# Folding the later batches' softmax into w_in with seven half-size products in place of eight

## The chip, the cores and the metric

The kernel runs on one core of a Trainium2 chip. The metric is device time in microseconds (us) of one execution, the median of several runs. The program uses five engines that run side by side, each in its own program order: TensorE (PE in the profile, with its weight loads as PEld), VectorE (DVE), ScalarE (ACT), GpSimd (POOL, here an issuer of DMAs) and SyncE (SP, likewise).

## What is computed

The reference is an attention over channels followed by a feed-forward layer. Its core, with 4 batches of 6080 tokens, 256 channels and 2048 hidden columns:

```python
qn = q / (np.linalg.norm(q, axis=1, keepdims=True) + 1e-06)
kn = k / (np.linalg.norm(k, axis=1, keepdims=True) + 1e-06)
s = kn.transpose(0, 2, 1) @ qn / tau            # 256 x 256 for each batch
a = softmax(s, axis=-1)
x = (v @ a).reshape(B * N, 256)
h = x @ w_in                                    # 256 -> 2048
r = np.maximum(h, 0.0)
g = s_moe * (r * r) + b
out = g @ w_out                                 # 2048 -> 256
```

The kernel never forms `v @ a`. It multiplies the softmax of a batch into `w_in` once, `wa = a @ w_in` (256 x 2048), and then computes `h = v @ wa`. The product `a @ w_in` is called the fold here, and the fold of batches 1, 2 and 3 is what the change touches.

## The kernel before

One long loop goes through 48 groups of 512 tokens, 16 steps to a group. A step is one pass of the loop: two matmuls of 128x512 for the hidden columns of the group at hand (`mm1`), and seven matmuls of 128x128 for the output of the group before. That output is computed by a seven-product scheme of its own (`seven_items`), whose results VectorE evacuates. On odd steps ScalarE evacuates two hidden tiles through a ReLU.

```python
    for s in range(NS + FT):
        g, m = divmod(s, FT)                # FT = 16
        if g < NG:
            mm1(g, m)                       # PE: 2 x 128x512
        ...
        if work:
            items, n = work[0]
            for f in items[:n]:             # PE: 7 x 128x128 (n = 7); an evacuation on DVE after each product
                f()
        ...
        if g < NG and m % 2 == 1:
            relu(g, m // 2)                 # ACT, out of h_ps (ps_h has 2 buffers)
        if g < NG and g not in plain and m in SQUARES:
            square(g, *SQUARES[m])          # m = 3, 5: ACT, one tile each; m = 8, 12: DVE, two tiles each
        ...
        elif m == 0 and 0 < g and g - 1 not in plain:
            square(g - 1, 6, 8, nc.vector)
        elif 0 < g and g - 1 not in plain and m in SUMS:
            sums_of(g - 1, SUMS[m])         # DVE, m = 2, 3, 6, 10
        for f in side.pop(s, []):           # whatever was put at this step
            f()
```

Each engine keeps the order in which the loop issues its instructions. The work of the next batch (its gram matrix, norms, softmax and fold) is put into this loop with `at_step`, in the steps before its first group. The finishing part starts 54 steps ahead of a point three steps before that group; for batch 1 these are the steps from 120 on, with its first group beginning at step 176:

```python
    FIN = (0, 3, 5, 7, 9, 11, 13, 17, 19, 22)
    ...
        w1 = first_group[b] * FT - 3        # 173 for batch 1
        fin_len = 54
        ...
        def fin_step(gr=gr, s=w1 - fin_len):
            ops = gr.finish_ops()
            for i, f in enumerate(ops):
                at_step(int(s) + 1 + (FIN[i] if i < len(FIN) else FIN[-1] + 3 * (i - len(FIN) + 1)), f)
```

The first ten of these operations are the copy of the gram matrix, the norms, four activations for the inverse norms, the scaling, two exponentials and the row sums. Then comes the fold: four blocks of 512 columns, two output halves each, so eight items, three steps apart (145, 148, ... 166 for batch 1):

```python
            def scaled(f0, n, m, wa_ps):
                dst = self.wa[:, m, ds(f0, n)]
                if m == 0 and not (self.b == 0 and NW <= f0 < 3 * NW):
                    po(nc.scalar.mul(out=dst, in_=wa_ps, mul=st["rs"][:, m : m + 1]))
                else:
                    po(nc.vector.tensor_scalar_mul(
                        out=dst, in0=wa_ps, scalar1=st["rs"][:, m : m + 1]))

            def fold_mm(f0, n, m, wa_ps):
                for j in range(CH):                          # CH = 2
                    po(nc.tensor.matmul(wa_ps, st["e"][:, j, ts(m, P)],
                                        w_in16[:, j, ds(f0, n)],
                                        start=(j == 0), stop=(j == CH - 1)))

            def fold_one(f0, n, m):
                def f():
                    wa_ps = self.bank("wa_ps", CH, C).rearrange("p a c -> p (a c)")[:, :n]
                    fold_mm(f0, n, m, wa_ps)
                    scaled(f0, n, m, wa_ps)
                return f
```

For batches 1 to 3 `self.bank` takes its tile from `ps_gram`, a pool with one buffer. An item therefore can begin on TensorE only when the evacuation of the item before it has ended. Even items are evacuated by ScalarE, odd ones by VectorE.

Of the kernel before, what the change touches and what calls it, by code (L numbers as in the profile page):

```python
# [9 lines left out]
FP16 = mybir.dt.float16  # L10
FP32 = mybir.dt.float32
FP32R = mybir.dt.float32r
AF = mybir.ActivationFunctionType
ALU = mybir.AluOpType
# [3 lines left out]
def kernel(  # L18
# [12 lines left out]
    nc = tc.nc  # L31
    P = 128

    B, N, C = q.shape
    Dff = moe_w_in.shape[1]
# [20 lines left out]
    def po(ins):  # L56

        tc.keep_in_program_order(ins)
        return ins

    def pool(name, bufs, **kw):
        return ctx.enter_context(tc.tile_pool(name=name, bufs=bufs, **kw))
# [3 lines left out]
    wpool = pool("wpool", 1)  # L66
    qk_pool = pool("qk_pool", 8)
    sq_pool = pool("sq_pool", 2)
    late_pool = pool("late_pool", NLATE)
    f3_pool = pool("f3_pool", 13)  # L70
    sm_pool = pool("sm", 1)
    apool = pool("apool", 2)
# [3 lines left out]
    gpool = pool("gpool", 2)  # L76
    spool = pool("spool", 1)
    upool = pool("upool", 4)
    opool = pool("opool", 2)

    ps_gram = pool("ps_gram", 1, space=PSUM)
# [29 lines left out]
    class Gram:  # L111
# [45 lines left out]
        def norm_ops(self, c):  # L157

            qc, kc = self.tiles[c]
            _, np_, jc = self.chunks[c]  # L160
            st = {}

            at_end = self.b == 0 and c >= len(self.chunks) - NLATE

            def squares(a, js):
                def f():
                    if "sq" not in st:
                        st["sq"] = (late_pool if at_end else sq_pool).tile(
                            [P, 2, JC, C], FP16, tag="sq", name="sq")
                    if a == 1 and at_end and c == len(self.chunks) - 1:  # L170
                        po(nc.vector.tensor_mul(
                            st["sq"][:np_, 1, js, :], kc[:np_, js, :], kc[:np_, js, :]))
                    elif a == 0 and (self.b > 0 or at_end or c % 2 == 0):
                        po(nc.vector.tensor_mul(  # L174
                            st["sq"][:np_, 0, js, :], qc[:np_, js, :], qc[:np_, js, :]))
                    else:
                        po(nc.scalar.activation(  # L177
                            out=st["sq"][:np_, a, js, :], in_=(qc, kc)[a][:np_, js, :],
                            func=AF.Square))
                return f  # L180

            def fold(half, arrays, last):
                def f():
                    src = st["f", 2 * half] if 2 * half < jc else st["sq"]
                    if ("f", half) not in st:
                        if last:
                            t = f3_pool.tile([P, 2, 1, C], FP16, tag="f3", name="f3")
                        else:
                            t = sq_pool.tile([P, 2, half, C], FP16, tag=f"f{half}", name="f")
                        st["f", half] = t  # L190
                    po(nc.vector.tensor_add(  # L191
                        st["f", half][:np_, arrays], src[:np_, arrays, :half, :],
                        src[:np_, arrays, half : 2 * half, :]))
                    if last and c == 0:
                        self.first = st["f", half]
                    if last and (c == 0 or self.b > 0 and c == len(self.chunks) - 1):
                        for rows in self.rows:
                            rows.append((st["f", half], np_, 1))
                return f

            def into_first():

                dst, src = self.first[:np_], st["f", 1][:np_]
                if self.b == 0:
                    po(nc.vector.tensor_add(dst, dst, src))
                else:
                    po(nc.gpsimd.dma_start(out=dst, in_=src, accum_op=ALU.add))  # L207

            def unfolded(a):
                self.rows[a].append((st["sq"], np_, jc))  # L210

            ops = []
            for h in range(0, jc, 4):
                js = slice(h, min(h + 4, jc))
                ops += [squares(1, js), squares(0, js)]
            if at_end:
                def rows(a):
                    if a == 0 or jc == 2:
                        return unfolded(a)
                    half = sq_pool.tile([P, 2, 2, C], FP16, tag="f2", name="half")  # L220
                    po(nc.vector.tensor_add(half[:np_, 1], st["sq"][:np_, 1, :2], st["sq"][:np_, 1, 2:]))
                    self.rows[1].append((half, np_, 2))
                return ops + [rows]
            if jc == 8:
                ops += [fold(4, slice(0, 1), False), fold(4, slice(1, 2), False)]
            ops += [fold(2, slice(0, 2), False), fold(1, slice(0, 2), True)]
            return ops + [into_first] if 0 < c < len(self.chunks) - 1 else ops
# [24 lines left out]
        def finish_ops(self):  # L252
# [78 lines left out]
            def first_block(n):  # L331

                two = [self.bank("wa_ps", CH, C)[:, 0, :n], h_tile("wa_ps")[:, 0, :n]]
                r_ps = self.bank("r_ps", CH, C)[:, :, 0]
                for j in range(CH):
                    exps(j)
                    for ch in range(CH):
                        po(nc.tensor.matmul(r_ps[:, ch : ch + 1], st["e"][:, j, ts(ch, P)],
                                            parts16, start=(ch == 0 and j == 0),
                                            stop=(ch == CH - 1 and j == CH - 1),  # L340
                                            skip_group_check=True))
                    for m in range(CH):
                        po(nc.tensor.matmul(two[m], st["e"][:, j, ts(m, P)],
                                            w_in16[:, j, :n],
                                            start=(j == 0), stop=(j == CH - 1)))
                st["rs"] = sm_pool.tile([P, CH], FP32, tag="rs", name="rs")
                po(nc.vector.reciprocal(out=st["rs"], in_=r_ps))
                for f0 in range(0, n, P):
                    for m in range(CH):
                        scaled(f0, P, m, two[m][:, ds(f0, P)])  # L350
# [5 lines that stand above are left out]
                    scaled(f0, n, m, wa_ps)  # L356
                return f

            if self.b == 0:
                blocks = [(2 * P, 2 * P), (4 * P, 2 * P), (6 * P, 2 * P), (2 * NW, NW), (3 * NW, NW)]  # L360
            else:
                blocks = [(f0, NW) for f0 in range(0, Dff, NW)]
            folds = [fold_one(f0, n, m) for f0, n in blocks for m in range(CH)]
            if self.b == 0:
                return [norms(1), *inverse(1), norms(0), *inverse(0), lambda: scale(CH),
                        lambda: first_block(2 * P)] + folds
            return [copy_out, norms_both, *inverse(), scale, lambda: exps(0), lambda: exps(1),
                    sums] + folds

        def bank(self, name, a, b):  # L370

# [189 lines left out]
        po(nc.scalar.copy(out=T[:, ts(i, 2), :], in_=w[:, 0, :, :P] if T is T2 else w[:, 0, :, P:]))  # L561


    side, early = {}, {}

    def at_step(s, f):
        side.setdefault(int(s), []).append(f)
# [31 lines left out]
    for b in range(1, B):  # L599
        gr = grams[b]  # L600
        w0 = first_group[b - 1] * FT + (26 if b == 1 else 6)
        w1 = first_group[b] * FT - 3
        NCH = len(gr.chunks)
        fin_len = 54
        span = (w1 - fin_len) - w0 - 12
        n = NCH * JC
        for c in range(NCH):
            sc = w0 + span * c * JC / n
            at_step(max(3, sc - 16), lambda gr=gr, c=c: gr.load(c))
            if c == 0:  # L610
                at_step(sc, gr.start)
            for j in range(JC):
                at_step(w0 + span * (c * JC + j) / n, lambda gr=gr, c=c, j=j: gr.mm(c, j))

            def norm_step(gr=gr, c=c, sc=sc):
                ops = gr.norm_ops(c)
                for i, f in enumerate(ops):
                    at_step(int(sc) + 2 + 1 + i * 3, f)
            at_step(sc + 1, norm_step)

        def fin_step(gr=gr, s=w1 - fin_len):
            ops = gr.finish_ops()
            for i, f in enumerate(ops):
                at_step(int(s) + 1 + (FIN[i] if i < len(FIN) else FIN[-1] + 3 * (i - len(FIN) + 1)), f)
        at_step(w1 - fin_len - 12, fin_step)


# [292 lines left out]
```

## Time and profile before

The time is 718.22 us, the median of three runs (718.15 to 718.64). The profiled execution spans 716.3 us with a mean granted TensorE clock of 0.997.

| group of instructions, per the profile | count | mean ns of one |
|---|---|---|
| fold matmul, 128x512 (`wa_ps`) | 56 | 379 |
| hidden matmul, 128x512 (`h_ps`) | 1408 | 379 |
| ReLU, 128x1024, ACT | 376 | 1022 |
| square of a hidden tile, 128x1024, ACT | 93 | 1052 |
| scaled fold evacuation, 128x512, ACT | 13 | 683 |
| scaled fold evacuation, 128x512, DVE | 15 | 744 |
| output evacuation, 128x256, DVE | 138 + 138 + 46 | 481, 477, 482 |
| sum of two f16 tiles, 128x2048, DVE | 45 | 1215 |
| square or sum of f16 tiles, 128x1024, DVE | 39 (L174) | 683 |

A mean duration is the time from an instruction's start to its end. Instructions of one engine overlap a little, so the spacing from start to start in a busy stretch is shorter and is read from the timeline. This matters most on TensorE, where a 128x512 matmul lasts 379 ns in the records and the next one starts 216 ns later. A "releaser" is the instruction whose end let a waiting one go.

### The profile page before, as it was taken

To read this page: it belongs to the slowest core of one execution; us is meant where nothing else is said; L and a number is where in the kernel's file an instruction comes from. 1 tells how busy PE (TensorE), PEld (TensorE's weight loads), DVE (VectorE), ACT (ScalarE), POOL (GpSimd) and SP (SyncE) were. 2 spreads that over 40 slices of the span, in tenths; PEclk is the share of its full clock that TensorE was granted. 3 is DMA by queue.
4 is the path that set the end of the run, shared out by engine and by line. 5 is a ranking of instruction groups with operands and counts; after the bars stand their busy time and mean duration, and the time that the engine had idled before them with its cause. 6 is when DMAs were issued, how large, how long until landed. Compare 5 with 4: busy or idle time off the path is not lost.

```text
span 716.3 us, 17491 instructions
## 1 busy us (share of the span) xinstructions
PE 696.8 (97%) x7421; PEld 503.6 (70%) x7421; DVE 624.0 (87%) x877; ACT 544.7 (76%) x592; POOL 110.8 (15%) x189
## 2 busy tenths in 40 slices
PE   4699999999999999999999999999999999999998
PEld 2456777776677777777677777777668777777777
DVE  4889999988789989998889899998887888888886
ACT  5779877787777777778777778777877777777874
POOL 4532332102101222101010222110000000000000
PEclk9999999999999999999999999999999999999999
DMA  9999999636565978444672887843323333321201
GB/s 236 207 259 167 165 174 136 122 89 124 111 122 109 135 134 144 112 89 95 138 146 52 145 137 125 153 90 77 98 63 75 94 70 75 97 60 46 82 31 75
DMA packets 87454, 83.47 MB, mean 117 GB/s; under 512 B 56304, under 2 KB 62256, under 8 KB 87376
## 3 DMA queue, kind: packets, MB, share of 16 engines
q0 software_dynamic: 26608, 43.40, 37.7%
q1 hardware_dynamic: 60192, 37.64, 22.0%
q8 instruction: 58, 0.95, 0.6%
q10 hardware_dynamic: 576, 1.31, 0.5%
q14 instruction: 20, 0.16, 0.1%
HBM read 78.91 MB, written 24.90 MB: 145 GB/s over the span
## 4 chain that ended last, share of the span: by engine, by line
PE 93%; DMA 3%; DVE 2%; ACT 2%; issue 0%; ACTq 0%; DVEq 0%
PE h_ps L658 45%; PE o_ps L826 40%; PE s_ps L148 4%; PE wa_ps L327 2%; DMA qk<-in_k_dram 1%; DMA raw<-in_q_dram 1%; ACT sq L177 1%; PE o_ps L730 1%; DVE f L191 1%; PE o_ps L704 0%; ACT r L668 0%; ACT r L269 0%; DVE sq L174 0%; PE n_ps L244 0%; DVE o_sb L686 0%
## 5 line engine op out<-in xcount | busy, mean ns | idle before, releaser
L668 ACT ACTIVATE r<-h_ps 128x1024 f16<-128x1024 f32 (+1 forms) x384 | 388.4, 1013 | 151.8 <-PE h_ps L658 148.1
L658 PE MATMUL h_ps<-vT,wa 128*128 128x512 f16 (+7 forms) x1632 | 452.2, 364 | 0.6 <-ACT wa L320 0.5
L826 PEld LDWEIGHTS <-S 128*128 128x128 f16 x2944 | 198.0, 98 | 84.8 <-issue 0.2
L826 PEld LDWEIGHTS <-g 128*128 128x128 f16 x2208 | 155.1, 98 | 74.1
L681 DVE TENSOR_TENSOR g<-r 128x2048 f16<-128x2048 f16 (+2 forms) x150 | 174.6, 1164 | 14.0 <-ACT r L668 13.6
L826 PE MATMUL o_ps<-T,S 128*128 128x128 f16 x2208 | 183.3, 219 | 0.1
L658 PEld LDWEIGHTS <-wa 128*128 128x128 f16 x1632 | 135.8, 98 | 20.6 <-ACT wa L320 0.8
L826 PE MATMUL o_ps<-w_out,g 128*128 128x128 f16 x1472 | 134.2, 219 | 0.2 <-DVE u L686 0.2
L686 DVE SCALAR_TENSOR_TENSOR o_sb<-o_ps,s_out,u 128x256 f32<-128x256 f32 x138 | 66.4, 481 | 50.9 <-PE o_ps L826 48.8
L679 ACT ACTIVATE g<-r 128x1024 f16<-128x1024 f16 (+1 forms) x97 | 100.4, 1035 | 0.2
L148 PE MATMUL s_ps<-qk 128*128 128x256 f16 (+1 forms) x384 | 71.7, 288 | 14.2 <-ACT qk L139 9.0
L386 POOL DMA_DIRECT2D v<-in_v_dram x48 | 31.0, 648 | 263.6 <-DMA vT<-v 187.0
L686 DVE SCALAR_TENSOR_TENSOR u<-o_ps,s_out,rowconst 128x256 f32<-128x256 f32 x138 | 65.8, 477 | 0.0
L826 PE MATMUL o_ps<-w_out,S 128*128 128x128 f16 x736 | 63.5, 219 | 0.0
L826 PE MATMUL o_ps<-N,g 128*128 128x128 f16 x736 | 63.4, 219 | 0.0
L207 POOL DMA_DIRECT2D f<-f x30 | 26.3, 876 | 224.3 <-DVE f L191 183.1
L755 DVE TENSOR_TENSOR S<-S,g 128x2048 f16<-128x2048 f16 (+1 forms) x47 | 56.4, 1201 | 1.3
L177 ACT ACTIVATE sq<-qk 128x1024 f16<-128x1024 f16 (+2 forms) x53 | 54.5, 1041 | 3.9 <-DMA qk<-in_k_dram 2.3
L753 DVE TENSOR_TENSOR S<-g 128x2048 f16<-128x2048 f16 (+1 forms) x47 | 56.0, 1192 | 0.0
L757 DVE TENSOR_TENSOR S<-g 128x2048 f16<-128x2048 f16 x46 | 55.9, 1215 | 0.0
L759 DVE TENSOR_TENSOR S<-g,S 128x2048 f16<-128x2048 f16 x46 | 55.8, 1214 | 0.0
L148 PEld LDWEIGHTS <-qk 128*128 128x128 f16 (+1 forms) x384 | 33.0, 103 | 20.8 <-ACT qk L139 9.5
(83 smaller groups left out, 313.9 us busy)
## 6 DMA issues: line engine op xcount, KB each, us to landing
out_dram<-o_sb SPq DMA_DIRECT2D x42, 512.0 KB, 2.9
v<-in_v_dram POOLq DMA_DIRECT2D x47, 256.0 KB, 4.9
qk<-in_k_dram POOLq DMA_DIRECT2D x42, 256.0 KB, 7.0
qk<-in_q_dram POOLq DMA_DIRECT2D x42, 256.0 KB, 7.7
f<-f POOLq DMA_DIRECT2D x30, 128.0 KB, 3.1
vT<-v SPq DMA_TRANSPOSE x182, 3.0
out_dram<-o_sb SPq DMA_DIRECT2D x10, 256.0 KB, 5.4
w<-in_moe_w_out_dram POOLq DMA_DIRECT2D x4, 512.0 KB, 10.1
```

Source lines behind the costliest of these rows:

```text
L148: po(nc.tensor.matmul(self.s_ps[:, ch, :], qc[:np_, j, ts(ch, P)], kc[:np_, j, :], start=(c == 0 and j == 0 and ch == 0), stop=(c == len(s ...
L177: po(nc.scalar.activation(out=st["sq"][:np_, a, js, :], in_=(qc, kc)[a][:np_, js, :], func=AF.Square))
L658: po(nc.tensor.matmul(dst, wa[:, ci, ts(m, P)], src, start=(ci == 0), stop=(ci == CH - 1), skip_group_check=True))
L668: po(nc.scalar.activation(out=r16[:, :, i % 2, :n], in_=h_tiles.pop((g, i))[:, :, :n], func=AF.Relu))
L679: po(nc.scalar.activation(out=dst, in_=src, func=AF.Square))
L681: po(nc.vector.tensor_mul(dst, src, src))
L686: po(nc.vector.scalar_tensor_tensor(out=dst, in0=src, scalar=s_out, op0=ALU.mult, in1=add, op1=ALU.add))
L753: po(nc.vector.tensor_add(T[1], A21, A22))
L755: po(nc.vector.tensor_sub(T[2], T[1], A11))
L757: po(nc.vector.tensor_sub(T[3], A11, A21))
L759: po(nc.vector.tensor_sub(T[4], A12, T[2]))
L826: po(nc.tensor.matmul(st[name][:, j, :], a()[:, i, ts(j, P)], w[:, i, :], start=first, stop=last, skip_group_check=True))
```

## The change

The fold of batches 1 to 3 uses the seven-product form of a 2x2 block product. Take A(m, k) as the four 128x128 blocks of the exponentials and B(k, n) as blocks of `w_in`, where n is the half of the 2048 columns. For a piece of 512 columns in each half (there are two such pieces, p = 0 and 1), the direct form needs eight matmuls of 128x512, two for each of the four outputs C(m, n). The new form needs seven. They use four sums of the A blocks (S1 to S4), which are made anew for each batch, and four sums of the B blocks (T1, T2, T3, N4), which depend only on `w_in` and are made once, during the finishing part of batch 1. These last take buffers that the first batch's last squares have left free, for which the pool of those buffers gets one tag for each buffer.

The four partial sums 1 to 4 share one PSUM tile and are accumulated in place: each product adds to what is there, and what is there is read in between. Products 1 to 3 are read out by ScalarE into f32 tiles (u1, u2, u3), product 4 by ScalarE into the output, and products 5, 6 and 7 by VectorE, which adds a u tile in the same instruction. The items now lie 2.4 steps apart, rounded down, in place of 3.

```diff
-    late_pool = pool("late_pool", NLATE)
+    late_pool = pool("late_pool", 1)
+    fold_pool = pool("fold_pool", 1)
 ... (the first batch's last squares now take one tag of late_pool each)
+            def half_sums():
+                A = lambda m, k: st["e"][:, k, ts(m, P)]
+                S = st["S"] = [fold_pool.tile([P, P], FP16, tag=f"S{n}", name=f"S{n}")
+                               for n in range(1, 5)]
+                po(nc.vector.tensor_add(S[0], A(1, 0), A(1, 1)))
+                po(nc.vector.tensor_sub(S[1], S[0], A(0, 0)))
+                po(nc.vector.tensor_sub(S[2], A(0, 0), A(1, 0)))
+                po(nc.vector.tensor_sub(S[3], A(0, 1), S[1]))
+
+            def seven_folds(p):
 ...
+                def product(a, w, then, new=False):
+                    def f():
+                        if new:
+                            st["wa_ps"] = self.bank("wa_ps", CH, C).rearrange("p a c -> p (a c)")
+                        po(nc.tensor.matmul(st["wa_ps"], a(), w(), start=new, stop=True,
+                                            skip_group_check=True))
+                        then()
+                    return f
+
+                def keep(n, m):
+                    def f():
+                        u[n] = fold_pool.tile([P, NW], FP32, tag=f"u{n}", name=f"u{n}")
+                        po(nc.scalar.mul(out=u[n], in_=st["wa_ps"], mul=rs(m)))
+                    return f
+
+                def out(m, n, k=None):
+                    def f():
+                        if k is None:
+                            po(nc.scalar.mul(out=C_(m, n), in_=st["wa_ps"], mul=rs(m)))
+                        else:
+                            po(nc.vector.scalar_tensor_tensor(
+                                out=C_(m, n), in0=st["wa_ps"], scalar=rs(m), op0=ALU.mult,
+                                in1=u[k], op1=ALU.add))
+                    return f
+
+                return [
+                    product(lambda: A(0, 0), lambda: B(0, 0), keep(1, 0), True),
+                    product(lambda: S(2), lambda: T("T2"), keep(2, 0)),
+                    product(lambda: S(3), lambda: T("T3"), keep(3, 1)),
+                    product(lambda: A(1, 1), lambda: T("N4"), out(1, 0)),
+                    product(lambda: A(0, 1), lambda: B(1, 0), out(0, 0, 1), True),
+                    product(lambda: S(1), lambda: T("T1"), out(1, 1, 3), True),
+                    product(lambda: S(4), lambda: B(1, 1), out(0, 1, 2)),
+                ]
 ...
             return [copy_out, norms_both, *inverse(), scale, lambda: exps(0), lambda: exps(1),
-                    sums] + folds
+                    sums_and_halves] + seven_folds(0) + seven_folds(1)
 ...
+    def w_in_sums(i):                       # F = Dff // 2 columns, 128x1024 each
 ...
+        po([lambda: nc.vector.tensor_sub(W["T1"], B(0, 1), B(0, 0)),
+            lambda: nc.vector.tensor_sub(W["T2"], B(1, 1), W["T1"]),
+            lambda: nc.vector.tensor_sub(W["T3"], B(1, 1), B(0, 1)),
+            lambda: nc.vector.tensor_sub(W["N4"], B(1, 0), W["T2"])][i]())
 ...
         def fin_step(gr=gr, s=w1 - fin_len):
+            if gr.b == 1:
+                for i in range(4):
+                    at_step(int(s) + 4 + 4 * i, lambda i=i: w_in_sums(i))
             ops = gr.finish_ops()
             for i, f in enumerate(ops):
-                at_step(int(s) + 1 + (FIN[i] if i < len(FIN) else FIN[-1] + 3 * (i - len(FIN) + 1)), f)
+                at_step(int(s) + 1 + (FIN[i] if i < len(FIN) else FIN[-1] + 2.4 * (i - len(FIN) + 1)), f)
```

The fold of batch 0 keeps the direct form.

More of the change, by code (lines that the diff above doesn't have):

```diff
@@ L167, in f @@
                     if "sq" not in st:
-                        st["sq"] = (late_pool if at_end else sq_pool).tile(
-                            [P, 2, JC, C], FP16, tag="sq", name="sq")
+                        if at_end:
+                            st["sq"] = late_pool.tile([P, 2, jc, C], FP16, tag=f"sq{c}", name="sq")
+                        else:
+                            st["sq"] = sq_pool.tile([P, 2, JC, C], FP16, tag="sq", name="sq")
                     if a == 1 and at_end and c == len(self.chunks) - 1:
@@ new lines, in seven_folds @@
+            def seven_folds(p):
+                A = lambda m, k: st["e"][:, k, ts(m, P)]
+                B = lambda k, n: w_in16[:, k, ds(n * (Dff // 2) + p * NW, NW)]
+                T = lambda n: W[n][:, ts(p, NW)]
+                S = lambda n: st["S"][n - 1]
+                C_ = lambda m, n: self.wa[:, m, ds(n * (Dff // 2) + p * NW, NW)]
+                rs = lambda m: st["rs"][:, m : m + 1]
+                u = {}
+                def product(a, w, then, new=False):
[15 more added lines that the diff above has]
+                            po(nc.scalar.mul(out=C_(m, n), in_=st["wa_ps"], mul=rs(m)))
+                        else:
+                            po(nc.vector.scalar_tensor_tensor(
[11 more added lines that the diff above has]
+                ]
@@ L359, in finish_ops @@
             if self.b == 0:
                 blocks = [(2 * P, 2 * P), (4 * P, 2 * P), (6 * P, 2 * P), (2 * NW, NW), (3 * NW, NW)]
[L361 to L364, printed above, removed]
+                folds = [fold_one(f0, n, m) for f0, n in blocks for m in range(CH)]
                 return [norms(1), *inverse(1), norms(0), *inverse(0), lambda: scale(CH),
@@ L366, in finish_ops, with sums_and_halves @@
                         lambda: first_block(2 * P)] + folds
+            def sums_and_halves():
+                sums()
+                half_sums()
             return [copy_out, norms_both, *inverse(), scale, lambda: exps(0), lambda: exps(1),
-                    sums] + folds
+                    sums_and_halves] + seven_folds(0) + seven_folds(1)
         def bank(self, name, a, b):
@@ L561, in cast_w @@
         po(nc.scalar.copy(out=T[:, ts(i, 2), :], in_=w[:, 0, :, :P] if T is T2 else w[:, 0, :, P:]))
+    W = {}
+    def w_in_sums(i):
+        F = Dff // 2
+        B = lambda k, n: w_in16[:, k, ds(n * F, F)]
+        if i == 0:
+            c0, c1, c2 = range(NCH0 - NLATE, NCH0)
+            W["T1"] = late_pool.tile([P, F], FP16, tag=f"sq{c1}", name="T1w")
+            W["T2"] = late_pool.tile([P, F], FP16, tag=f"sq{c2}", name="T2w")
+            both = late_pool.tile([P, 2, F], FP16, tag=f"sq{c0}", name="TNw")
+            W["T3"], W["N4"] = both[:, 0], both[:, 1]
+        po([lambda: nc.vector.tensor_sub(W["T1"], B(0, 1), B(0, 0)),
+            lambda: nc.vector.tensor_sub(W["T2"], B(1, 1), W["T1"]),
+            lambda: nc.vector.tensor_sub(W["T3"], B(1, 1), B(0, 1)),
+            lambda: nc.vector.tensor_sub(W["N4"], B(1, 0), W["T2"])][i]())
     side, early = {}, {}
```

## The prediction

> **What bounds the kernel now.** I read the page first: busy shares, then the chain that ended last.
>
> ```profile
> PE 696.8 (97%) x7421; PEld 503.6 (70%) x7421; DVE 624.0 (87%) x877; ACT 544.7 (76%) x592; POOL 110.8 (15%) x189
> PE 93%; DMA 3%; DVE 2%; ACT 2%; issue 0%; ACTq 0%; DVEq 0%
> ```
>
> TensorE is busy 97% of the span, and 93% of the chain lies on it. So any time that TensorE gains or loses goes straight into the result. Next I asked for busy time by stretches. The columns are: stretch, length, busy time and count of PE, PEld, DVE, ACT and POOL, granted clock, DMA share, GB/s.
>
> ```profile
> 147.00:196.00 49.00, 49.00 (x524) 34.26 (x523) 41.43 (x55) 37.87 (x44) 7.41 (x14) 1.00 0.54 106
> ```
>
> This stretch holds the finishing of batch 1, and TensorE has no gap in it. VectorE has 7.6 us to spare, ScalarE 11.1 us. On average there is room for added work; whether there is room at the right moment is read from timelines. TensorE's timeline around one fold item (start, length, line, count):
>
> ```profile
> 169.86 0.59 PE L327 MATMUL wa_ps<-w_in,eT 128*128 128x512 f16 x2
> 170.29 0.59 PE L658 MATMUL h_ps<-vT,wa 128*128 128x512 f16 x2
> 170.72 0.28 PE L826 MATMUL o_ps<-w_out,g 128*128 128x128 f16 x2
> ...
> 172.76 0.59 PE L327 MATMUL wa_ps<-w_in,eT 128*128 128x512 f16 x2
> ```
>
> From the first start to the second, two 128x512 matmuls take 0.43 us, or 0.216 each. From fold to fold is 2.90 us: three steps and one fold, so a bare step is (2.90 - 0.43) / 3 = 0.823 us. ScalarE's timeline there:
>
> ```profile
> 167.69 0.68 ACT L320 ACTIVATE wa<-wa_ps,rs 128x512 f16<-128x512 f32 x1
> 168.84 1.02 ACT L668 ACTIVATE r<-h_ps 128x1024 f16<-128x1024 f32 x1 [0.48 <-PE h_ps L658]
> 169.76 1.05 ACT L679 ACTIVATE g<-r 128x1024 f16<-128x1024 f16 x1
> 170.92 1.02 ACT L668 ACTIVATE r<-h_ps 128x1024 f16<-128x1024 f32 x1
> 171.84 1.05 ACT L679 ACTIVATE g<-r 128x1024 f16<-128x1024 f16 x1
> 172.79 1.01 ACT L668 ACTIVATE r<-h_ps 128x1024 f16<-128x1024 f32 x1
> ...
> 186.03 0.68 ACT L320 ACTIVATE wa<-wa_ps,rs 128x512 f16<-128x512 f32 x1
> 186.60 1.02 ACT L668 ACTIVATE r<-h_ps 128x1024 f16<-128x1024 f32 x1
> ```
>
> From start to start a ReLU takes 0.92 us, a square 0.95, a fold evacuation 0.57; the evacuation is complete after 0.68. The reader is to see that around two of every eight ReLUs ScalarE also has two squares, and there it runs without a gap. VectorE's timeline, later in the same fold:
>
> ```profile
> 177.60 0.48 DVE L686 SCALAR_TENSOR_TENSOR o_sb<-o_ps,s_out,u 128x256 f32<-128x256 f32 x1 [0.34 <-PE o_ps L826]
> 178.00 1.22 DVE L681 TENSOR_TENSOR g<-r 128x2048 f16<-128x2048 f16 x1
> ...
> 181.94 1.22 DVE L681 TENSOR_TENSOR g<-r 128x2048 f16<-128x2048 f16 x1
> 183.08 0.74 DVE L322 TENSOR_SCALAR wa<-wa_ps,rs 128x512 f16<-128x512 f32 x1
> 183.74 0.48 DVE L686 SCALAR_TENSOR_TENSOR o_sb<-o_ps,s_out,rowconst 128x256 f32<-128x256 f32 x1
> ```
>
> Start to start an output evacuation takes 0.40 us, a square 1.14, a fold evacuation 0.66 (complete after 0.75).
>
> **What the Trainium skill says.** "ScalarE: Activation LUTs", section "What ACT_TABLE_LOAD costs", gives an activation with one per-partition operand as 280 ns plus 0.833 ns per column, and says that back-to-back ones overlap by 93 ns. For 512 columns that is 707 ns; the trace has 683, and 0.68 against 0.57 above is an overlap of 0.11. "VectorE: DVE Perf Modes", section "Why PSUM operands drop a tier", holds an f32 PSUM source to one element per cycle. The trace agrees: 744 ns for 512 columns out of PSUM. An added f32 operand should then cost nothing more: the existing multiply-and-add of 128x512 out of PSUM (L686) takes 745 ns. "Perfetto Trace Analysis", section "Identifying Performance Opportunities", asks for gaps on the engine that should be saturated and for what each waits on. Here there are none before the change, so I look for those it makes.
>
> **The change part by part.**
>
> *TensorE, removed.* Sixteen matmuls of 128x512 per batch become fourteen: 2 x 0.216 = 0.43 us, three times, 1.30 us.
>
> *VectorE and ScalarE, added.* ScalarE evacuates eight products per batch where it had four: 4 x 0.57 = 2.3 us. VectorE evacuates six where it had four, 1.3 us, and makes four 128x128 sums. From the sums of 1024 and 2048 columns (683 and 1215 ns, so 0.52 us per 1024 and 0.15 fixed) I estimate 0.2 us each, 0.8 in all. Both fit the 11.1 and 7.6 us to spare.
>
> *Moved: the waits.* Every product must wait until the one before it is evacuated, as before. But the spacing falls from 3 steps to 2.4, cut to whole steps, and products 1 to 4 all go to ScalarE. In batch 1 the fourteen products fall on steps 144, 146, 149, 151, 154, 156, 158, 161, 163, 166, 168, 170, 173 and 175. I lay this out on the trace's clock with the spacings above. A product is readable 0.43 us after its start (0.38 duration and 0.05, the lag that the ReLU rows show behind their matmul); the same 0.05 goes behind an evacuation.
>
> Step 144 ends where step 145's hidden matmul now starts, at 166.13. Product 1 starts there; product 2 follows two steps later, 166.13 + 0.22 + 1.65 = 168.00; product 3 at 168.00 + 0.22 + 2.47 = 170.68; product 4 is due at 172.54. ScalarE: evacuation of 2 at 168.43, ReLU 169.00, square 169.92, ReLU 170.87, square 171.79, and only then the evacuation of 3, at 172.74. It is complete at 173.42, so product 4 starts at 173.48. **TensorE stands for 0.94 us.**
>
> From 173.48, product 5 starts at 176.16, product 6 at 178.02, and product 7 is due at 179.88. VectorE must first do the output evacuation of step 156 (177.60 in the trace, shifted to about 177.89, since five single folds and the wait make 2.02 us where four double folds made 1.73) and the square (178.29), so it evacuates product 6 at 179.43, complete at 180.18. Product 7 starts at 180.23: **0.35 us lost**.
>
> Product 8 starts at 182.92, 9 at 184.78, 10 at 187.46, and 11 is due at 189.33. The next two squares meet the evacuations again. ScalarE runs ReLU 184.60, square 185.52, evacuation 186.47, ReLU 187.04, square 187.96, evacuation of 10 at 188.91, complete 189.59. Product 11 starts at 189.64: **0.31 us**. That ReLU delay also reaches VectorE through the next square, and product 14 waits for the evacuation of 13, due 196.05, free 196.22: **0.17 us**.
>
> Together 1.77 us lost against 0.43 saved: +1.34 us per batch. The three batches begin at the same place in a group (steps 176, 368 and 560 are multiples of 16), so this happens three times: +4.0 us.
>
> *The sums of w_in.* Four of 683 ns on VectorE, at steps 123, 127, 131 and 135 of batch 1 only. The first two fall before an idle 1.25 us at 152.97 and are absorbed. The last two fall into a run that the timeline shows gapless, but for 0.19 us, from 155.12 to 165. They add 2 x 0.61 and so push the evacuation at 161.37 by 1.03, to end near 162.9; the output product that reuses its PSUM bank starts at 162.41 in the trace. Loss about 0.5 us, once.
>
> Sum: 718.22 + 4.0 + 0.5 = 722.7 us. I choose this number, since every spacing in it stands in the trace.
>
> **The rivals.**
>
> 1. *The saving comes through*, no wait appears: 718.22 - 1.30 = 716.9 us. For it: the average room above. Against it: the gapless run of ReLU, square, ReLU, square stands in the trace, with one evacuation queued behind it and one matmul behind that.
> 2. *ScalarE becomes the bound of the fold*: late ReLUs hold the two hidden buffers and stop `mm1` as well. By my layout the ReLU queued behind evacuation 3 starts at 173.31, and its buffer is needed about 1.5 us after that, so I expect no such wait. If spacings are 0.1 longer than read, each long wait grows by some 0.3 us: about 725 us.
> 3. *The next batch's first hidden matmul waits for the last evacuation* (step 175 against 176). The columns that product 14 writes are first read at step 188, so I expect nothing; if the dependence covered the whole tile, 1 us per batch, 725 to 726 us.
> 4. *The startup changes* through the new buffer tags. The sizes and order are the same; nothing speaks for it.
>
> **Range and chances.** A layout error of 0.3 us in each batch's waits moves the sum by 1 us. Longer waits (rivals 2 and 3) and absorbed ones (a third of the waits vanishing gives 720.9) are about as likely, so 720.3 to 724.5. Two percent is 14 us, far beyond any of these: within 2% at 0.98, each side 0.01.
>
> **What the profile after would show.** TensorE idle or held at a fold matmul, released by ScalarE's `u` evacuation about 0.9 us, once per batch, at the fourth product; smaller waits at the seventh, eleventh and fourteenth, by VectorE, ScalarE and VectorE; six fold matmuls fewer; about 0.5 us of output-product waits on VectorE near 158 and 162 us. The stretch of each fold would be longer by 1.3 us. The prediction is wrong if product 4 starts within 0.2 us of product 3's due spacing, if a multiply-and-add with an f32 operand takes clearly more than 745 ns, or if the spans outside the folds move.

## The result and the profile after

The changed kernel takes 722.56 us (median of six runs, 722.39 to 722.65) where the kernel before takes 718.21. The ratio is 1.006, 95% interval 1.0047 to 1.0073: a loss of 4.35 us. The prediction named 722.7 us, so what is left to learn is whether the loss arises where and as it said.

The page of the changed kernel, busy time and the chain that ended last:

```profile
PE 699.0 (97%) x7415; PEld 504.0 (70%) x7415; DVE 632.6 (88%) x899; ACT 551.3 (76%) x604; POOL 111.1 (15%) x189
PE 87%; ACT 6%; DVE 3%; DMA 3%; issue 1%; ACTq 0%; DVEq 0%
```

TensorE runs 7415 matmuls where it ran 7421: the six saved are there. But the chain lies on TensorE for 87% of the span and no longer for 93%, and ScalarE has 6% of it where it had 2%. Work that used to run beside TensorE now stands in its way.

The same stretch of time as before, with the same columns:

```profile
147.00:196.00 49.00, 47.71 (x504) 33.03 (x502) 44.07 (x62) 39.22 (x47) 6.75 (x13) 1.00 0.51 104
```

TensorE was busy for the whole 49.00 us and now leaves 1.29 us open. The modelled ends of matmuls cover the first part of each wait, so the true loss is larger; it is better read from start times. ScalarE is still idle for 9.8 us of this stretch, VectorE for 4.9 us. Neither has become the bound by volume.

TensorE's timeline of the fold of batch 1, only the fold matmuls (start, length, line; the bracket is the idle time that the profile shows and its releaser):

```profile
171.43 0.38 PE L386 MATMUL wa_ps<-TNw,S 128*128 128x512 f16 x1
...
174.20 0.38 PE L386 MATMUL wa_ps<-TNw,eT 128*128 128x512 f16 x1 [0.75 <-ACT u L394]
...
178.74 0.38 PE L386 MATMUL wa_ps<-T1w,S 128*128 128x512 f16 x1
...
180.94 0.38 PE L386 MATMUL wa_ps<-w_in,S 128*128 128x512 f16 x1 [0.17 <-DVE wa L402]
...
188.16 0.38 PE L386 MATMUL wa_ps<-TNw,S 128*128 128x512 f16 x1
...
190.32 0.38 PE L386 MATMUL wa_ps<-TNw,eT 128*128 128x512 f16 x1
...
194.87 0.38 PE L386 MATMUL wa_ps<-T1w,S 128*128 128x512 f16 x1
...
196.87 0.38 PE L386 MATMUL wa_ps<-w_in,S 128*128 128x512 f16 x1
```

Two steps and one product take 2 x 0.823 + 0.216 = 1.86 us when nothing is waited for. From the third to the fourth product it is 2.77, so 0.91 us are lost; from the sixth to the seventh 2.20, so 0.34; from the tenth to the eleventh 2.16, so 0.30. From the thirteenth (194.87) to the fourteenth (196.87) it is 2.00, so 0.14. The sum is 1.69 us, and batches 2 and 3 show the same four spacings within 0.01 us. Each of the last three starts 0.04 to 0.06 us after the read-out of the product before it has ended: VectorE's at 180.88, ScalarE's at 190.28, VectorE's at 196.81. The bracket of 0.75 is smaller than 0.91 because it counts only from the modelled end of the matmul before.

ScalarE's timeline ahead of the longest wait:

```profile
170.65 1.06 ACT L759 ACTIVATE g<-r 128x1024 f16<-128x1024 f16 x1
171.60 1.03 ACT L748 ACTIVATE r<-h_ps 128x1024 f16<-128x1024 f32 x1
172.50 1.07 ACT L759 ACTIVATE g<-r 128x1024 f16<-128x1024 f16 x1
173.45 0.70 ACT L394 ACTIVATE u<-wa_ps,rs 128x512 f32<-128x512 f32 x1
```

The third product started at 171.43; with the prediction's 0.43 us its result could be read at 171.86. ScalarE took it at 173.45, after a ReLU and a square that stand ahead in its program order. It was done at 174.15, and the fourth product started at 174.20.

The last part of the loss lies ahead of the fold. Each group's output is made by seven products of 16 matmuls, and the timeline cuts across them. TensorE's timeline at the output products in the kernel before, then in the changed kernel, and VectorE's in the changed kernel:

```profile
159.89 0.50 PE L826 MATMUL o_ps<-T,S 128*128 128x128 f16 x6
160.22 0.22 PE L826 MATMUL o_ps<-w_out,g 128*128 128x128 f16 x1
```

```profile
158.44 0.73 PE L906 MATMUL o_ps<-T,S 128*128 128x128 f16 x7
...
160.26 0.50 PE L906 MATMUL o_ps<-T,S 128*128 128x128 f16 x6
160.97 0.22 PE L906 MATMUL o_ps<-w_out,g 128*128 128x128 f16 x1 [0.21 <-DVE u L766]
```

```profile
157.71 0.68 DVE L638 TENSOR_TENSOR TNw<-w_in 128x1024 f16<-128x1024 f16 x1
158.31 0.48 DVE L766 SCALAR_TENSOR_TENSOR u<-o_ps,s_out,rowconst 128x256 f32<-128x256 f32 x1
158.71 0.68 DVE L297 TENSOR_TENSOR sm_t<-sm_t,rNone 128x512 f32<-128x512 f32 x1
159.31 1.22 DVE L837 TENSOR_TENSOR S<-g 128x2048 f16<-128x2048 f16 x1
160.44 0.48 DVE L766 SCALAR_TENSOR_TENSOR u<-o_ps,s_out,rowconst 128x256 f32<-128x256 f32 x1
```

Seven output matmuls usually take 0.55 us; here they take 0.73. The third product of the group begins with the fifth of the seven, which was due at 158.66; it waits for the evacuation begun at 158.31, behind the third sum of w_in, which ends at 158.79. That is 0.18 us. The next wait ends at 160.97, right after the evacuation begun at 160.44: six matmuls of 0.056 from 160.26 would have ended their issue at 160.60, so 0.37 us. The fourth product begins there; before the change its spacing was 0.33 us, and here it is 0.71. Together 0.55 us.

The account closes: three batches of 1.69 us, plus 0.55, minus six matmuls of 0.216 (1.30), is 4.32 us against 4.35 measured. The two profiled executions differ by 4.5 us (720.8 against 716.3), 0.18 of it at the startup.

### The profile page after: what moved, and what is told of

The parts are those of the page before. It is cut to its first block, busy times and chain, and to the rows that moved or that the text cites. A ratio compares the mean times of both kernels' runs of the same rounds, so it can differ in the third digit from the quotient of the medians.

```text
span 720.8 us, 17509 instructions
## 1 busy us (share of the span) xinstructions
PE 699.0 (97%) x7415; PEld 504.0 (70%) x7415; DVE 632.6 (88%) x899; ACT 551.3 (76%) x604; POOL 111.1 (15%) x189
## 4 chain that ended last, share of the span: by engine, by line
PE 87%; ACT 6%; DVE 3%; DMA 3%; issue 1%; ACTq 0%; DVEq 0%
PE h_ps L738 42%; PE o_ps L906 37%; PE s_ps L149 4%; ACT g L759 2%; ACT r L748 2%; DMA qk<-in_k_dram 1%; DMA raw<-in_q_dram 1%; PE wa_ps L386 1%; ACT u L394 1%; ACT sq L180 1%; PE o_ps L810 1%; DVE f L194 1%; PE o_ps L784 0%; DVE o_sb L766 0%; PE wa_ps L330 0%
## 5 line engine op out<-in xcount | busy, mean ns | idle before, releaser
L748 ACT ACTIVATE r<-h_ps 128x1024 f16<-128x1024 f32 (+1 forms) x384 | 388.9, 1015 | 147.5 <-PE h_ps L738 144.0
```

Source lines behind the costliest of these rows:

```text
L748: po(nc.scalar.activation(out=r16[:, :, i % 2, :n], in_=h_tiles.pop((g, i))[:, :, :n], func=AF.Relu))
```

## The experiments

Three explanations had to be told apart. The *queue theory* is that of the prediction: a product waits for an evacuation that stands behind other work in its engine's order. The *work theory* says that the added evacuations and sums cost because there are more of them, wherever they stand. The *in-place theory* says that reading a PSUM tile (the tile that a matmul writes) between two products that accumulate into it costs. Product 7 adds to product 6's tile in the same way as products 1 to 4 share theirs. The kernel before took 718.26 us beside the first four runs and 718.30 beside the last four.

**The third read-out on VectorE.** This is u3 in each of the two pieces, so products 3 and 10 of a batch.

```diff
-                        po(nc.scalar.mul(out=u[n], in_=st["wa_ps"], mul=rs(m)))
+                        if n == 3:
+                            po(nc.vector.tensor_scalar_mul(out=u[n], in0=st["wa_ps"], scalar1=rs(m)))
+                        else:
+                            po(nc.scalar.mul(out=u[n], in_=st["wa_ps"], mul=rs(m)))
```

> Only the read-out of the third product (u3) goes to VectorE; the steps, the seven products and all sums stay as in the change. Queue theory (the loss is TensorE waiting for the evacuation that stands behind ReLU and square in ScalarE's order): the wait at the fourth product, 0.91 us in each batch, goes, and so does the one at the eleventh, 0.30; waits of about 0.2 and 0.3 us at the sixth and seventh product of the first piece stay. From 722.56 us to about 719.0. Work theory (the added evacuations cost the same on whichever engine they run): no gain, 722.3 to 722.8, since the same number of evacuations is made. In-place theory (reading a PSUM tile that is being accumulated is what costs): no gain either, the third product is still read between two products.

Measured: 718.88 us, ratio 1.0008 (1.0000 to 1.0017). The timeline of TensorE in this kernel, third and fourth product, and of VectorE:

```profile
171.33 0.38 PE L386 MATMUL wa_ps<-TNw,S 128*128 128x512 f16 x1
...
173.19 0.38 PE L386 MATMUL wa_ps<-TNw,eT 128*128 128x512 f16 x1
```

```profile
171.64 0.48 DVE L769 SCALAR_TENSOR_TENSOR u<-o_ps,s_out,rowconst 128x256 f32<-128x256 f32 x1
172.03 0.74 DVE L395 TENSOR_SCALAR u<-wa_ps,rs 128x512 f32<-128x512 f32 x1
```

The spacing is 1.86 us, that of no wait. Work and reading are as many as in the change, and 3.7 of its 4.35 us are gone. VectorE's evacuation is the longer one (0.74 against 0.70 us); it is only taken at once. Two smaller waits stay, 0.15 us at the sixth product and 0.32 at the seventh; those at the eleventh and fourteenth are gone too.

**The sums of w_in at other steps.**

```diff
-                    at_step(int(s) + 4 + 4 * i, lambda i=i: w_in_sums(i))
+                    at_step(int(s) + (4, 8, 9, 24)[i], lambda i=i: w_in_sums(i))
```

> The four sums of w_in move from steps 123, 127, 131, 135 of batch 1 to 123, 127, 128, 143, where VectorE has idle time; all else as in the change. Queue theory: the third and fourth sum no longer delay the output evacuations near 158 and 162 us, so about 0.45 us come back, 722.1 us, and the stretches of batches 2 and 3 stay as they are. Work theory: the sums cost their 2.7 us of VectorE wherever they are, so no change, 722.5.

Measured: 722.46 us, ratio 1.0057 (1.0044 to 1.0070), a miss: 0.10 us came back by the medians, not 0.45. The interval is too wide to settle so small a difference, but the trace settles it: TensorE's starts, set against those of the kernel before, slip by 0.07 us near 157, where a product waits for a sum that VectorE ends at 156.95, and by 0.26 near 160.7. So 0.33 us of the 0.55 are left. The third sum, three steps earlier than in the change, still pushes the run of VectorE that follows, and the fourth output product still waits for the same evacuation, now from 160.25. The places that I took for free were free only for the two sums that were there already.

**The old fold, closer together.**

```diff
-                at_step(int(s) + 1 + (FIN[i] if i < len(FIN) else FIN[-1] + 3 * (i - len(FIN) + 1)), f)
+                at_step(int(s) + 1 + (FIN[i] if i < len(FIN) else FIN[-1] + 2.4 * (i - len(FIN) + 1)), f)
```

This is the kernel before with nothing changed but the spacing.

> The kernel before, with its eight direct items of two matmuls and its own evacuations, only 2.4 steps apart in place of 3. Queue theory: spacing and place alone make waits, about 0.56 us at the fourth item and 0.13 at the seventh in each batch, 718.2 + 3 x 0.69 = 720.3 us. In-place theory and work theory: no new evacuation and no in-place reading, so 718.2 us.

Measured: 720.28 us, ratio 1.0028 (1.0017 to 1.0039). TensorE's timeline, third and fourth item:

```profile
171.65 0.59 PE L327 MATMUL wa_ps<-w_in,eT 128*128 128x512 f16 x2
174.27 0.59 PE L327 MATMUL wa_ps<-w_in,eT 128*128 128x512 f16 x2 [0.38 <-ACT wa L320]
```

They are 2.62 us apart, where two steps and one item of two matmuls make 2.08: 0.54 us lost, by ScalarE (and 0.12 at the seventh item), in the kernel that has no in-place reading and not one evacuation more. About half of the change's loss can thus be had without the seven products at all.

**The seven products on chosen steps.** The third read-out is on VectorE as in the first run, the sums are spread as in the second, and the steps are listed:

```diff
+    SEVEN = (24, 26, 29, 32, 35, 37, 39, 41, 44, 47, 49, 51, 53, 57)
-                at_step(int(s) + 1 + (FIN[i] if i < len(FIN) else FIN[-1] + 2.4 * (i - len(FIN) + 1)), f)
+                at_step(int(s) + 1 + (FIN + SEVEN)[i], f)
```

> The seven-product fold with its fourteen products on chosen steps (24, 26, 29, 32, 35, 37, 39, 41, 44, 47, 49, 51, 53, 57 after the start in place of multiples of 2.4), the third read-out on VectorE, and the sums of w_in spread as in the run before. Queue theory: no product finds its predecessor unread, so only the six saved matmuls remain: 718.2 - 1.3 + 0.1 = 717.0 us, below the kernel before. Work theory: all evacuations and sums are still made, so well above the kernel before, about 722.

Measured: 717.25 us, ratio 0.9986 (0.9980 to 0.9993). This is below both kernels. The stretch of the fold of batch 1 in this kernel:

```profile
147.00:196.00 49.00, 48.91 (x524) 34.13 (x522) 46.48 (x67) 39.10 (x46) 7.41 (x14) 1.00 0.59 108
```

TensorE is busy 48.91 of 49.00 us, with VectorE fuller than in the change (46.48 against 44.07). All products, sums and evacuations are made, and each of the fourteen products of batch 1 starts within 0.02 us of its due spacing. Of the 0.25 us by which it misses the expected 717.0, the sums of w_in explain 0.23: they cost 0.33 us and not 0.1, as in the run with the sums at other steps.

**The sums of w_in alone.** The old fold with its old spacing; the four sums at the steps of the change, and nothing reads them.

> The fold is that of the kernel before (eight items of two matmuls, 3 steps apart); only the four sums of w_in are made, at the steps of the change, and nothing reads them. Queue theory: the two output-product waits seen in the profile of the change (about 0.2 us near 158, where the third product of a group waits for the first's evacuation, and about 0.35 near 161) appear here too, 718.25 + 0.55 = 718.8 us, all of it in batch 1. Rival, the sums are free and the half microsecond comes with the seven products: 718.25.

Measured: 718.83 us, ratio 1.0008 (1.0000 to 1.0016), 0.53 above the kernel before. Its trace shows the same two waits, the second one released by the same evacuation:

```profile
158.47 0.73 PE L904 MATMUL o_ps<-T,S 128*128 128x128 f16 x7
...
161.00 0.22 PE L904 MATMUL o_ps<-w_out,g 128*128 128x128 f16 x1 [0.21 <-DVE u L764]
```

So the half microsecond belongs to the sums, and comes with the old fold as well.

**Two steps apart.** The change with 2 in place of 2.4.

> The change with its products 2 steps apart in place of 2.4; nothing else differs. Queue theory: the waits grow and move, to about 0.44, 0.97, 0.33, 0.34 and 0.85 us at the fifth to eighth and the fourteenth product of a batch, 2.93 us against 1.7; saved matmuls and sums as before: 726.2 us. Work theory: the same work is done, 722.5.

Measured: 726.33 us, ratio 1.0111 (1.0097 to 1.0125). TensorE's timeline, the products that waited:

```profile
174.60 0.38 PE L386 MATMUL wa_ps<-w_in,eT 128*128 128x512 f16 x1 [0.28 <-ACT wa L400]
177.43 0.38 PE L386 MATMUL wa_ps<-T1w,S 128*128 128x512 f16 x1 [0.82 <-DVE wa L402]
179.62 0.38 PE L386 MATMUL wa_ps<-w_in,S 128*128 128x512 f16 x1 [0.17 <-DVE wa L402]
181.80 0.38 PE L386 MATMUL wa_ps<-w_in,eT 128*128 128x512 f16 x1 [0.16 <-DVE wa L402]
...
193.81 0.38 PE L386 MATMUL wa_ps<-w_in,S 128*128 128x512 f16 x1 [0.69 <-DVE wa L402]
```

By start times the five lose 0.45, 0.97, 0.33, 0.32 and 0.85 us, 2.92 in all, on the products that had been named. Three times 2.92, plus 0.55, minus 1.30 is 8.01 us, against 8.03 measured. Note that the wait at the fourth product is gone: one step earlier, the third read-out comes ahead of the second square. The loss does not simply grow with closeness; it depends on what stands in the queue at that step.

**Other steps, nothing else.** All evacuations are on the engines of the change, and the sums of w_in are where it has them.

```diff
+    SEVEN = (24, 25, 31, 33, 35, 37, 39, 40, 42, 44, 47, 50, 55, 57)
-                at_step(int(s) + 1 + (FIN[i] if i < len(FIN) else FIN[-1] + 2.4 * (i - len(FIN) + 1)), f)
+                at_step(int(s) + 1 + (FIN + SEVEN)[i], f)
```

> The change with all evacuations on the engines that it has and the sums of w_in where it has them; only the steps of the fourteen products differ: 24, 25, 31, 33, 35, 37, 39, 40, 42, 44, 47, 50, 55, 57. Queue theory: about 0.35 us of waits are left in each batch against 0.43 saved, plus the 0.55 of the sums: 718.5 us. Work theory (the evacuations on ScalarE and the f32 read-outs cost wherever they stand): 722.5.

Measured: 718.49 us, ratio 1.0003 (0.9995 to 1.0012). The same instructions on the same engines, 4.1 us faster than in the change. The trace shows 0.33 us of waits left in batch 1, at the second, fourth, eighth and fourteenth product. This decides against the work theory and the in-place theory.

**The sums of w_in on GpSimd.** The placed version, with `nc.gpsimd.tensor_sub` for the four sums, all at steps 123 to 129.

> The placed seven-product fold (717.25 us) with the four sums of w_in made by GpSimd, which is busy 15% of the span, in place of VectorE. Queue theory: the 0.33 us that the sums still cost in batch 1 goes, 716.9 us. Rival: GpSimd's arithmetic takes so long that products 2 or 3 wait for their sums, or it holds up VectorE's operations beside it: 717.3 us or more.

Measured: 723.27 us, ratio 1.0070 (1.0057 to 1.0082): 6 us slower than with VectorE, a miss. GpSimd's timeline and VectorE's in this kernel:

```profile
136.50 2.37 POOL L639 TENSOR_TENSOR T1w<-w_in 128x1024 f16<-128x1024 f16 x1
138.95 2.99 POOL L640 TENSOR_TENSOR T2w<-w_in,T1w 128x1024 f16<-128x1024 f16 x1
```

```profile
137.04 2.92 DVE L765 TENSOR_TENSOR g<-r 128x2048 f16<-128x2048 f16 x1
139.88 2.60 DVE L194 TENSOR_TENSOR f<-sq 112x1024 f16<-112x1024 f16 x1
142.40 0.86 DVE L770 SCALAR_TENSOR_TENSOR o_sb<-o_ps,s_out,u 128x256 f32<-128x256 f32 x2
```

GpSimd's sums take 2.37 to 3.10 us each. Beside them VectorE's square takes 2.92 us where it takes 1.21 at the same place in the kernel before, and the addition of 112x1024 takes 2.60 where it takes 0.68. TensorE then stands idle for 3.53 us ahead of an output product, released by VectorE, and it is slower for a while after that. Its timeline, and the busy times of the stretch that follows, with the columns used above:

```profile
142.93 0.37 PE L910 MATMUL o_ps<-N,g 128*128 128x128 f16 x2 [3.53 <-DVE o_sb L770]
143.10 1.06 PE L742 MATMUL h_ps<-vT,wa 128*128 128x512 f16 x2
143.95 0.95 PE L910 MATMUL o_ps<-N,g 128*128 128x128 f16 x7
```

```profile
143.00:146.30 3.30, 3.30 (x21) 2.18 (x20) 3.30 (x3) 1.02 (x1) 3.30 (x2) 0.50 0.00 0
```

The granted TensorE clock was 0.50 in this stretch, and two hidden matmuls took 0.85 us from start to start where they usually take 0.43; from 146.30 on the clock is 1.00 again. That the stall brings the lower clock on is not shown; it follows the stall. By start times TensorE loses 3.69 us at the stall, 1.61 from there to 146.30, and 0.88 at 149.39, where an output product waits for a sum of VectorE that comes late. That makes 6.18; less the 0.41 that the placed version loses in the same part, it is 5.77. The first product starts 5.74 us later than in the placed version (172.31 against 166.57), nearly the whole loss. It was not the products that waited for their sums: the last sum ended at 147.5.

## Why the prediction was right

*What bounds the kernel.* Right. Every wait that TensorE gained appeared in the total, and the account closes to 0.03 us.

*The saving.* Right: six matmuls fewer, and the placed version gets their 1.30 us, less the 0.33 of the sums.

*The added work beside the path.* Right on average, and the average had no part in the result. The multiply-and-add with an f32 operand has a median of 745 ns, as read from the existing 128x512 one. The sums of 128x128 take 0.20 to 0.23 us. One size was a little off: ScalarE's read-outs into the output as the fourth product last 714 ns by their median where 683 was assumed, 0.03 us on products that nothing waited for.

*The waits.* Right in place, engine and size. Predicted were 0.94, 0.35, 0.31 and 0.17 us at products 4, 7, 11 and 14; measured are 0.91, 0.34, 0.30 and 0.14. The layout used the trace's spacings, start to start, and not the durations, and followed the program order of both engines. One of its readings was loose: ScalarE did not run quite without a gap before, since the ReLU at 170.92 starts 1.16 us after the square ahead of it, where 0.95 is the spacing. In the change that gap is gone. That moving steps alone (718.49 us), or one read-out alone (718.88 us), takes the loss away shows that the waits are its cause.

*The sums of w_in.* Right in size (0.5 predicted, 0.55 measured), mostly wrong in place, so the agreement in size is in part luck: the one wait that was worked out did not come, and two others add up to nearly the same. (Its list of what the profile would show did expect waits near 158 and 162; they end near 158.8 and 161.0.) The step that failed said that the evacuation pushed from 161.37 holds the output product that starts at 162.41. The traces of the change and of the sums alone show the waits one and two evacuations earlier: the third output product waits for the first evacuation (0.18 us), the fourth for the second (0.37). The fourth product writes one half of a PSUM tile whose other half that evacuation reads. The prediction counted only reuse of the same half. The evacuation that it named was pushed as it said and ended at 163.04, but by then TensorE was late enough not to wait: its product started at 163.16.

*The rivals.* The saving without a wait did not come in the change, and came in the placed version. Late ReLUs did not stop the hidden matmuls, and the last evacuation did not hold the next batch: the only releasers of waits in the fold were the evacuations of products. Nothing shows a changed startup: the first of batch 0's later fold items starts at 37.61 us before and at 37.79 in the change, but the other seven traces with the new buffer tags have it between 37.5 and 37.9, and the one other trace with the old tags at 38.1. One thing in the prediction did not fit together: its range ended at 724.5, while its second and third rival were put at 725 to 726. As neither came, nothing hung on it.

## What to carry to other kernels

Where one engine is full, an instruction saved on it is worth what it costs only if the work that takes its place is already done when that engine arrives; count the queue that stands ahead of each evacuation, in program order and with start-to-start spacings, before counting idle shares. When a serial chain through a single buffer is laid between periodic work, choose its steps by hand against that period: the same instructions gave 722.56 us at an even 2.4 steps and 718.49 us on other steps. Try the other engine for the one evacuation that waits, even if it is the slower engine.

## What the runs showed of the hardware

I had not expected how much arithmetic on GpSimd slows VectorE. "SBUF — State Buffer" of the Trainium skill, section "SBUF: two separate sides", says that the two share a pair of ports as an exclusive lock, and that a VectorE operation with two SBUF inputs and a GpSimd operation that reads SBUF block each other for a whole instruction. The trace agrees, in turns: GpSimd's first sum ends at 138.87 us, and VectorE's waiting square 1.09 us later, at 139.96, nearly the 1.21 that it takes alone. GpSimd's second sum ends 1.98 us after that, at 141.94, and VectorE's addition 0.54 us after that. The next pair goes the same way: VectorE's square ends 1.08 us after GpSimd's third sum, and the fourth sum 1.98 us after the square. So most of the 2.92 and 2.60 us is waiting. The two multiply-and-adds, with one of their tensor inputs from PSUM, ran beside the third sum and took 0.86 us together, no longer than elsewhere. Eleven microseconds of such sums, on an engine that is idle 85% of the span in the kernel before, cost 6 us of the span, of which 1.61 fell into the stretch of 3.3 us with a granted clock of 0.50.
